# The experts' loops turned round: weight units outside, token pairs inside, both layers by seven products

## The chip, the cores and the metric

The program runs on one core of a Trainium2 chip. The metric is the device time in microseconds (us) of one execution; the time of before is the median of three runs. The trace belongs to one profiled execution. Names: PE in a row is TensorE's matmuls and PEld its weight loads, DVE is VectorE, ACT is ScalarE, POOL is GpSimd, SP is the engine whose queue issues every DMA of this program.

## The reference

Pooled attention over four batches, a dense layer pair with g = h cos h, and a mixture of eight experts whose token weights P come out of eight rounds of row and column normalization:

```python
k_p = k.reshape(B, H, Sp, pool, D).mean(axis=3)      # B, H, S, D = 4, 8, 576, 64; pool = 8
v_p = v.reshape(B, H, Sp, pool, D).mean(axis=3)
attn = softmax(scale * q @ k_p.T); x = (attn @ v_p)  # x: 2304 tokens x 512
h = x @ w_in; x = (h * np.cos(h)) @ w_out            # d_ff = 2048
logits = x @ w_gate; P = np.exp(logits - logits.max())
for _ in range(8):
    P /= P.sum(1, keepdims=True) + 1e-09
    P /= P.sum(0, keepdims=True) + 1e-09
    P *= N / E
for e in range(E):                                   # E = 8, F = 1024
    out += P[:, e:e + 1] * (np.maximum(x @ w1[e], 0.0) @ w2[e])
```

## The kernel before, in words

Every large product is made to fp32 accuracy out of three matmuls in the rounded fp32r type: each operand is cut into a high piece (a rounding copy on ScalarE) and a low piece (source minus high, on VectorE or GpSimd; `halves`), and high x high, high x low and low x high are added in PSUM. Tokens lie in six blocks of 384 (`NB`), and in the experts two blocks make one of three **pairs** (0, 1, 2). The experts' weights lie in 16 **units** (`NU`): half an expert, 512 hidden columns of `w1` and the rows of `w2` that belong to them. One pair through one unit is a **step**; there are 48.

Layer one of a step is a Strassen-Winograd product: seven products P1 to P7 in the order `ORDER`, for two halves h of the unit, each product 6 matmuls of 128x384 (`first_layer`, L1148 before, L1132 after). They need seven combinations of the weights (`w1_pieces`) and seven of the tokens (`x_pieces`), each with a high and a low piece. Layer two goes two ways before: `plain_layer` (L1267) multiplies with the eight plain products, 24 matmuls of 128x256 for each of six token tiles, and `strassen_layer` (L1287) uses seven products, 42 matmuls for each of three tile pairs, but needs seven combinations of the hidden values (`strassen_result`) and of `w2` (`w2_pieces`). VectorE adds the result into `acc` (`accumulate`).

The loops before: pairs outside, units inside. Pair 0 runs through all 16 units with layer two plain; on the way `w1_pieces` and `w2_pieces` make the seven combinations of every unit and store them to DRAM (`w1c`, `w2c`). Pairs 1 and 2 run through all units with layer two by seven products and read 14 + 14 pieces of 256 KB back in each step (`w1_cached`, `w2_cached`). The token pieces of a pair are made once at its start and stay in SBUF.

A planner (`Graph.schedule`) writes the order of each engine's instructions: every node has costs, a due time (`goal`, from which `latest` works back) and buffers from pools of named slots; the order on each engine is fixed once the program is built, and on the chip each engine runs its list in order and waits on semaphores. The string `STRASSEN` says how the 14 products of layer one (`a`) are mixed with those of layer two of the step before it (`0`, `1`, `2`: the three tile pairs).

Ahead of the experts come the attention and the dense layers (`hidden1`, `output1`), in which a weight piece of float64 input is converted by a chain of VectorE instructions, and the pooled keys and values of batches 1 to 3 are made by halving additions on VectorE and GpSimd (`load_k`, `load_v`: `kr`, `ks`, `vr`, `vs`). The gate's logits (`logits`: `pl`, then `pq`) and the normalization (`normalization`: `rw`, `cs`, `pc`, `cr`) are mixed into the end of the dense layers and the start of the experts.

Of the kernel before, what the change touches and what calls it, by code (L numbers as in the profile page):

```python
# [20 lines left out]
POOL = 8  # L21
# [42 lines left out]
class Slot:  # L64

    def __init__(self, tag):
        self.tag, self.free, self.holder, self.kinds = tag, 0.0, None, []


class Group:  # L70

    def __init__(self, graph, name, side, after=()):
        self.graph, self.name, self.side, self.after = graph, name, side, after
        self.kinds, self.pools, self.stack, self.users, self.closed = [], {}, None, 0, False

    def ready(self):
        return self.stack is not None or all(g.users == 0 for g in self.after)
# [14 lines left out]
class Kind:  # L92

    def __init__(self, group, pool, slots, strict=False):
        self.group, self.pool, self.slots, self.strict = group, pool, slots, strict
        self.queue = []
# [18 lines left out]
class Graph:  # L115
# [8 lines left out]
    def group(self, name, side="left", after=()):  # L124
        return Group(self, name, side, after)

    def kind(self, group, pool, names, strict=False):
        group.pools.setdefault(pool, None)
        slots = [self.slots.setdefault((pool, n), Slot(n)) for n in names]
        return Kind(group, pool, slots, strict)  # L130
# [7 lines left out]
    def add(self, engine, us, run, reads=(), writes=(), port=False, table=None, size=0, goal=FAR, name=None):  # L138
# [5 lines left out]
        for items, write in ((reads, False), (writes, True)):  # L144
            for item in items:
# [8 lines left out]
                if buf not in node.bufs:  # L154
                    node.bufs.append(buf)
                    buf.left += 1
                    if buf.kind:
                        buf.kind.group.users += 1
# [15 lines left out]
    def rank(self):  # L174
        self.latest()
        for node in self.nodes:
            if node.engine == ("PE",):
                continue
            for buf in node.bufs:
                store = node.engine == ("SP",)  # L180
                if buf.kind and (store or buf.kind.pool == "ps"):
# [5 lines left out]
        self.latest()  # L187
        for node in self.nodes:
            for buf in node.new:
                buf.first = min(n.late for n, _, _ in buf.acc)  # L190
                buf.kind.queue.append(buf)
                for slot in buf.kind.slots:
                    if buf.kind not in slot.kinds:
                        slot.kinds.append(buf.kind)
        for kind in {id(b.kind): b.kind for n in self.nodes for b in n.new}.values():
            kind.queue.sort(key=lambda b: b.first)

    def place(self, node):

        at, taken = 0.0, []  # L200
        for buf in node.bufs:
# [3 lines left out]
            if not kind.group.ready():  # L205
                return None
# [5 lines left out]
            for slot in kind.slots:  # L212
                if slot.holder is None and slot not in taken and (best is None or slot.free < best.free) and all(
# [9 lines left out]
    def schedule(self, log=None):  # L223
# [25 lines left out]
        while left:  # L249
# [38 lines left out]
            for buf in node.bufs:  # L288
# [3 lines left out]
                kind.group.open()  # L292
                kind.queue.remove(buf)
                slot = slots.pop(0)
                slot.holder, buf.slot = buf, slot
                buf.tile = kind.group.pools[kind.pool].tile(buf.shape, buf.dtype, tag=f"{kind.pool}{slot.tag}", name=buf.name)
# [13 lines left out]
            for buf in node.bufs:  # L310
                buf.left -= 1
                buf.end = max(buf.end, end)
                if buf.kind:
                    buf.kind.group.users -= 1
# [17 lines left out]
    def stuck(self, ready):  # L332
        kinds = {id(b.kind): b.kind for n in self.nodes for b in n.new}
        for k in kinds.values():
            if all(x.holder for x in k.slots):
                print(k.pool, [x.tag for x in k.slots], [(x.holder.name, x.holder.left) for x in k.slots],
# [39 lines left out]
def fused_kernel(ctx: ExitStack, tc: tile.TileContext, qT, kT, vT, v0, wa1, wb1, wa2, wb2, wg, out):  # L376
# [3 lines left out]

    base = g.group("base")
# [4 lines left out]
    late = g.group("late", "right", (second,))  # L386
    plain = g.group("plain", "left", (second,))
    last = g.group("last", "left", (plain, first))
    psum = g.group("psum")

# [6 lines left out]
    xtag = {n: g.kind(base, "xp", [n], True) for n in [f"{p}{j}" for j in range(NBLK) for p in ("xh", "xl")]}  # L397
    k_raw64 = g.kind(base, "xp", ["xh4", "xl4", "xh5", "xl5"], True)
    k_w = many(base, "wp", 19, True)
    k_raw = many(first, "rawp", 3, True)  # L400
    k_gh, k_gl = many(first, "gph", 6), many(first, "gpl", 6)
    k_acc = many(second, "accp", 4)
# [8 lines left out]
    k_gc = {n: g.kind(mid, "gc", [n]) for n in ("ones", "wgr", "wg2", "sel", "lg", "pr")}  # L411
    k_sk = {n: g.kind(mid, "sk", [n]) for n in ("lt", "m1", "m2", "nm", "rw", "cs", "cr")}
    k_tmp = many(mid, "tmp", 4)
    k_s5, k_c22, k_t5 = many(late, "cps", 2), many(late, "cpc", 1), many(late, "cpt", 3)
    k_w2 = many(late, "wp2", 18, True)
    k_gh2, k_gl2 = many(plain, "gph2", 7), many(plain, "gpl2", 7)
    GB = 18
    k_gbh, k_gbl = many(last, "gbh", GB), many(last, "gbl", GB)

# [37 lines left out]
    x1f_tile = dram.tile([NBLK, P, KC, NB], F32, name="x1f")  # L457
    w1c = dram.tile([NU, len(ORDER), P, 2, 2, HD], F32, name="w1c")
    w2c = dram.tile([NU, len(ORDER), 2, P, FU], F32, name="w2c")
    kept_wa = {(u, i, k): g.kept(None) for u in range(U1) for i in range(2 * FC) for k in range(2)}  # L460
    kept_x = {j: g.kept(None) for j in range(NBLK)}
    kept_w1 = {(u, n, k): g.kept(None) for u in range(NU) for n in ORDER for k in range(2)}
    kept_w2 = {(u, n, k): g.kept(None) for u in range(NU) for n in ORDER for k in range(2)}
# [80 lines left out]
    def pool_first_v(tiles):  # L544
# [12 lines left out]
        vpool[0] = vs  # L557

    def load_k(b):
        ks = buf(k_ks, [P, HP, SP], F32, "ks")  # L560
# [4 lines left out]
        kbd = kbds[b % 2]  # L565
        for j in range(2):
            activate(HP * SP, lambda j=j: kbd[j * D:(j + 1) * D, :, j * SP:(j + 1) * SP],
                     lambda j=j: ks[j * D:(j + 1) * D], reads=[ks], writes=[kbd])
        kpool[b] = kbd

    def load_v(b):
        vs = buf(k_vs, [SP, H, D], F32, "vs")
# [45 lines left out]
    x1 = {}  # L618
# [171 lines left out]
    def output1(j, u, c, gs, w, acc, nxt):  # L790
# [17 lines left out]
        if nxt:  # L808
            halves(NB, a, (acc, c), lambda k: nxt[k][:, c, :], [(t, c) for t in nxt])
            if j > 1:  # L810
                load(lambda: x1f_tile[j, :, c], a, P * NB * 4, reads=[(acc, c)], writes=[(kept_x[j], c)])
# [29 lines left out]
    accs, weights, waiting = {}, {}, []  # L841
# [6 lines left out]
    for task, (gi, u, j) in enumerate(tasks):  # L848
# [17 lines left out]
        if u == 0:  # L866
            accs[j] = buf(k_acc, [P, KC, NB], F32, "acc")
# [7 lines left out]
        if u == U1 - 1:  # L875
            x1[j] = x_tiles(j)
        waiting += [lambda c=c, j=j, u=u, gs=gs, w=w, a=accs[j]: output1(
            j, u, c, gs, [w[FC + f] for f in range(FC)], a, x1[j] if u == U1 - 1 else None) for c in range(KC)]
# [4 lines left out]
    gate = {n: buf(k_gc[n], s, d, n) for n, s, d in (  # L883
        ("ones", [P, P], F32), ("wgr", [P, KC, E], F32), ("wg2", [P, KC, P], F32R), ("sel", [G2 + E, E], F32),
        ("lg", [P, NT, E], F32), ("pr", [P, NT, E], F32))}
    ones, wgr, wg2, sel, lg, pr = (gate[n] for n in ("ones", "wgr", "wg2", "sel", "lg", "pr"))
    add("V", 0.17, lambda: nc.vector.memset(ones.tile, 0.0 + 1.0), [], [ones])
    load(lambda: wgr.tile, lambda: wg, P * KC * E * 4, writes=[wgr])
    add("G", 0.6, lambda: nc.gpsimd.memset(wg2.tile.bitcast(F32), 0.0), [], [wg2], port=True)
    activate(KC * E, lambda: wg2[:, :, :E], lambda: wgr.tile, reads=[wgr], writes=[wg2])  # L890
    add("V", 0.2, lambda: nc.vector.tensor_tensor(out=wg2[:, :, G2:G2 + E], in0=wgr.tile, in1=wg2[:, :, :E].bitcast(F32),
                                                  op=ALU.subtract), [wgr], [wg2], port=True)
    add("V", 0.17, lambda: nc.vector.tensor_tensor(out=sel.tile, in0=ident.tile[:G2 + E, :E],
                                                   in1=ident.tile[:G2 + E, G2:G2 + E], op=ALU.add), [], [sel], port=True)
# [4 lines left out]
    def logits(j, goal):  # L899

        pl = buf(b_g, [P, NB], F32, "pl")

        def run():
            for c in range(KC):
                for part in range(2):
                    nc.tensor.matmul(out=pl.tile, lhsT=wg2[:, c, :], rhs=x1[j][part][:, c, :],
                                     start=(c + part == 0), stop=(c == KC - 1 and part == 1))

        lt = sk("lt", [G2 + E, NB])
        pe(mm(2 * KC, NB), run, [wg2, *x1[j]], [pl, (lt, "room")], goal=goal)  # L910
        add("V", two(NB), lambda: nc.vector.tensor_copy(out=lt.tile, in_=pl[:G2 + E, :]), [pl], [lt])
        pq = buf(b_g, [P, TPB, E], F32, "pq")

        def turn():
            for i in range(TPB):
                nc.tensor.matmul(out=pq[:, i, :], lhsT=lt[:, i * P:(i + 1) * P], rhs=sel.tile, start=True, stop=True)

        pe(0.4, turn, [lt, sel], [pq], goal=goal + 3.5)
# [508 lines left out]
```

## Time and profile before

| | |
|---|---|
| time, median of 3 runs | 1992.84 us (1992.48 to 1993.19) |
| the profiled execution, its own time | 1993.46 us, its span 1991.7 us |
| busy in the span | PE 1942.5 us, PEld 1910.8, DVE 1427.6, ACT 961.4, POOL 284.1 |
| start (attention, dense layers) | to about 526 us |
| pair 0, units 0 to 15 | about 526 to 1052 us |
| pairs 1 and 2 | about 1052 to 1992 us |
| HBM read, written | 331.89 MB, 142.08 MB |

A busy PE is not PE at its peak, since matmuls overlap; how fast it goes is read from the distance of their starts. The profiled execution's own time is 1.8 us over its span and 0.6 us over the median.

### The profile page before, as it was taken

Reading aid. Unit: us, or ns where it says so; the run is one execution under the profiler, and the core shown is the slowest. Engines: PE = TensorE matmul, PEld = TensorE weight load, DVE = VectorE, ACT = ScalarE, POOL = GpSimd, SP = SyncE. Lnnn points to the kernel's source line nnn. Section 1 sums busy time; section 2 is a strip of 40 time slices with the busy share of each in tenths; the row PEclk is TensorE's granted clock in tenths of the full one; section 3 lists DMA queues with packets and bytes.
Section 4 is the critical chain, followed back from the end, with each engine's and each line's share of the span. In section 5 each row is a group of like instructions: output and inputs, shape, how many; then the busy total and the mean of one; then the engine's idle time right before and its main releaser. Section 6 shows DMA issues by size and latency. Waiting matters only on the chain.

```text
span 1991.7 us, 35651 instructions
## 1 busy us (share of the span) xinstructions
PE 1942.5 (98%) x13220; PEld 1910.8 (96%) x13220; DVE 1427.6 (72%) x2625; ACT 961.4 (48%) x2026; POOL 284.1 (14%) x249
## 2 busy tenths in 40 slices
PE   6799999999999999999999999999999999999998
PEld 4689999999999999999999999999999999999998
DVE  8898887645688877787776666666667666666666
ACT  6565445643444444444444445445445445444543
POOL 3452232200234232212120000000000000000000
PEclk9799999999999999999999999999999999999999
DMA  7447643334597988989888677678668667767863
GB/s 265 148 154 251 203 149 110 112 118 138 190 316 268 331 296 296 312 295 316 286 314 303 231 260 269 226 251 279 230 240 303 242 234 269 258 230 258 272 223 119
DMA packets 276461, 476.35 MB, mean 239 GB/s; under 512 B 27680, under 2 KB 90912, under 8 KB 276288
## 3 DMA queue, kind: packets, MB, share of 16 engines
q1 hardware_dynamic: 276288, 474.08, 69.5%
q8 instruction: 104, 1.70, 0.4%
q14 instruction: 69, 0.57, 0.1%
HBM read 331.89 MB, written 142.08 MB: 238 GB/s over the span
## 4 chain that ended last, share of the span: by engine, by line
PE 93%; DVE 5%; ACT 1%; DMA 1%; issue 0%; SPq 0%; DVEq 0%; ACTq 0%
PE py L1148 15%; PE pc L1287 13%; PE po L1267 13%; PE qc L1287 10%; PE px L1148 10%; PE pv L1148 10%; PE po L765 3%; PE ph L765 3%; PE po L767 3%; PE ph L766 3%; PE ph L767 3%; PE po L766 3%; PE psc L590 1%; DVE at L449 1%; PE ptr L684 1%; PE px L698 1%
## 5 line engine op out<-in xcount | busy, mean ns | idle before, releaser
L1287 PE MATMUL pc<-wc,gh 128*128 128x256 f32 x1536 | 280.5, 279 | 0.0
L1287 PEld LDWEIGHTS pc<-wc,gh 128*128 128x128 f32 x1536 | 238.2, 188 | 0.0
L1148 PE MATMUL py<-xc,wc 128*128 128x384 f32 x1152 | 232.0, 336 | 0.7 <-ACT py L442 0.7
L1287 PE MATMUL qc<-wc,gh 128*128 128x256 f32 x1152 | 215.6, 280 | 1.1 <-DVE qc L449 1.1
L1287 PE MATMUL pc<-wc,gl 128*128 128x256 f32 x768 | 214.6, 279 | 0.0
L1148 PEld LDWEIGHTS py<-xc,wc 128*128 128x128 f32 x1152 | 197.8, 188 | 1.4 <-ACT py L442 0.9
L1287 PEld LDWEIGHTS qc<-wc,gh 128*128 128x128 f32 x1152 | 186.5, 188 | 2.6 <-DVE qc L449 1.7
L449 DVE TENSOR_TENSOR gl<-sf,gh 128x384 fp32r<-128x384 f32 x256 | 137.6, 551 | 58.3 <-ACT gh L442 55.7
L1287 PE MATMUL qc<-wc,gl 128*128 128x256 f32 x576 | 161.8, 281 | 0.0
L1148 PE MATMUL pv<-xc,wc 128*128 128x384 f32 x768 | 154.6, 336 | 0.0
L1148 PE MATMUL px<-xc,wc 128*128 128x384 f32 x768 | 154.3, 335 | 0.0
L1267 PE MATMUL po<-vhi,gh 128*128 128x256 f32 x768 | 152.0, 279 | 0.7 <-DVE acc L1251 0.7
L1267 PE MATMUL po<-vlo,gh 128*128 128x256 f32 x768 | 152.1, 280 | 0.0
L1267 PE MATMUL po<-vhi,gl 128*128 128x256 f32 x768 | 151.7, 279 | 0.0
L1287 PEld LDWEIGHTS pc<-wc,gl 128*128 128x128 f32 x768 | 144.3, 188 | 0.0
L765 PE MATMUL po<-gh,wc 128*128 128x384 f32 x384 | 132.5, 345 | 7.0 <-ACT wc L442 7.0
L765 PE MATMUL ph<-xh,wc 128*128 128x384 f32 x384 | 133.0, 346 | 3.7 <-DVE r L449 3.7
L767 PE MATMUL ph<-xh,wc 128*128 128x384 f32 x384 | 130.8, 341 | 0.8 <-DVE wc L449 0.8
L766 PE MATMUL ph<-xl,wc 128*128 128x384 f32 x384 | 130.8, 341 | 0.1
L767 PE MATMUL po<-gh,wc 128*128 128x384 f32 x384 | 129.8, 338 | 0.8 <-DVE wc L449 0.8
L1148 PEld LDWEIGHTS pv<-xc,wc 128*128 128x128 f32 x768 | 130.4, 188 | 0.0
L1148 PEld LDWEIGHTS px<-xc,wc 128*128 128x128 f32 x768 | 130.2, 188 | 0.0
(209 smaller groups left out, 4588.9 us busy)
## 6 DMA issues: line engine op xcount, KB each, us to landing
wc<-w1c SPq DMA_DIRECT2D x448, 256.0 KB, 5.2
wc<-w2c SPq DMA_DIRECT2D x448, 256.0 KB, 5.4
wc<-wac SPq DMA_DIRECT2D x112, 256.0 KB, 4.9
w1c<-whi SPq DMA_DIRECT2D x112, 256.0 KB, 4.4
w1c<-wlo SPq DMA_DIRECT2D x112, 256.0 KB, 4.2
w2c<-vhi SPq DMA_DIRECT2D x112, 256.0 KB, 5.0
w2c<-vlo SPq DMA_DIRECT2D x112, 256.0 KB, 4.1
raw<-wa SPq DMA_DIRECT2D x48, 512.0 KB, 5.6
```

What stands on the lines that cost most here:

```text
L449: (nc.gpsimd if e == "G" else nc.vector).tensor_tensor(out=out(), in0=in0(), in1=in1(), op=op)
L590: nc.tensor.matmul(out=ps[off:off + n, 2 * hh:2 * hh + 2, :].rearrange("p h s -> p (h s)"), lhsT=qc()[:, hh, off:off + n], rhs=kpool_at[b] ...
L684: nc.tensor.transpose(ps[:, h, :], at[:, i, h, :], ident.tile)
L698: nc.tensor.matmul(out=px[e * D:(e + 1) * D, off:off + n], lhsT=vs[b][:, 2 * hp + e, :], rhs=pt[:, 2 * hh + e, off:off + n], start=True, s ...
L765: nc.tensor.matmul(out=ps, lhsT=lh, rhs=rh, start=(i == 0), stop=False)
L766: nc.tensor.matmul(out=ps, lhsT=lh, rhs=rl, start=False, stop=False)
L767: nc.tensor.matmul(out=ps, lhsT=ll, rhs=rh, start=False, stop=(i == total - 1))
L1148: nc.tensor.matmul(out=ps(), lhsT=l[:, k], rhs=r[:, c, :], start=(start and c + n == 0), stop=(c + n == 3), skip_group_check=True)
L1267: nc.tensor.matmul(out=po[:, d * HD:(d + 1) * HD], lhsT=l[:, r], rhs=w[f % 2, d][k][:, (f // 2) * HD:(f // 2 + 1) * HD], start=(f + n + d ...
L1287: nc.tensor.matmul(out=ps, lhsT=l[:, r], rhs=m[:, k], start=(start and h + n == 0), stop=(h + n == 3), skip_group_check=True)
```

## The change

1. The loops are turned round: units outside, pairs (1, 0, 2) inside. `w1_pieces` and `w2_pieces` run once for a unit and their 14 + 14 pieces stay in SBUF for three steps, in exactly 14 + 14 slots (`W1`, `W2`), so the next unit's pieces take the slots one by one as the last step lets go of them. Nothing of the weights is stored or reloaded.
2. All 48 steps use `strassen_layer`; `plain_layer` is gone. The output sums of all three pairs stay in SBUF (`k_acc2`).
3. The seven token pieces of each pair are stored to DRAM (`xc`, 768 KB each) and read again in every step but the first, into 7 slots (`x_loaded`).
4. The logits are fp32 matmuls of 8 columns straight out of `acc`, 12 for each block, in place of 8 fp32r matmuls of 384 columns, a copy and 3 small matmuls.
5. Keys and values of batch 1 are pooled on TensorE (`ON_PE`: `pk`, `pv`).
6. The planner works its due times out four times over, counting when a slot's next holder comes; slots of several pools can be joined; the dense layers' weights get 21 slots for 19.

```diff
+    W1, W2, GB, XR, T5 = 14, 14, 12, 7, 2
+    k_x = g.kind(base, "xp", xnames[:XR], True)
+    k_w1 = many(base, "wp", W1, True)
+    k_w = g.join(k_w1, many(second, "wq", 7), strict=True)
+    k_w2 = many(ahead, "wp2", W2, True)
...
+        if b in ON_PE:
+            tiles = load_rows(k1[ON_PE.index(b)])
+            pk = buf(b_a, [P, HP, SP], F32, "pk")
...
+                        nc.tensor.matmul(out=pk[:, hp, :], lhsT=t[:rows, i, hp * P:(hp + 1) * P], rhs=band[:rows, o:o + SP],
+                                         start=(c == 0), stop=(c == len(tiles) - 1))
...
-            for c in range(KC):
-                for part in range(2):
-                    nc.tensor.matmul(out=pl.tile, lhsT=wg2[:, c, :], rhs=x1[j][part][:, c, :],
...
+            for i in range(TPB):
+                for c in range(KC):
+                    nc.tensor.matmul(out=pl[:, i, :], lhsT=accs[j][:, c, i * P:(i + 1) * P], rhs=wgr[:, c, :],
...
         cut("P1", a11)
+        cut("P4", a22)
+        combine(a22, a21, a22, ALU.add)
+        cut("P5", a22)
+        combine(a21, a11, a21, ALU.subtract)
+        combine(a22, a22, a11, ALU.subtract)
+        cut("P6", a22)
         cut("P2", a12)
         cut("P7", a21)
+        combine(a12, a12, a22, ALU.subtract)
         cut("P3", a12)
-    def w1_cached(u):
...
+    def x_loaded(pair):
+        x = {}
+        for name in ORDER:
+            t = buf(k_x, [P, 2, 2, NB], F32R, "xc")
+            load(lambda t=t: t.tile.bitcast(F32), lambda name=name: xc[pair, ORDER.index(name)], P * 4 * NB * 4,
+                 reads=[kept_x[pair, name]], writes=[t])
...
-    def plain_layer(pair, u, gs, w, acc2, goals):
...
-    steps = [(pair, u) for pair in range(NTP) for u in range(NU)]
+    steps = [(u, pair) for u in range(NU) for pair in (1, 0, 2)]
...
+    for n, (u, pair) in enumerate(steps):
+        if pair == steps[0][1]:
+            w1, w2 = w1_pieces(u), w2_pieces(u)
+        pieces = {}
+        first_layer(w1, ready if n == 0 else x_loaded(pair), strassen_result(pieces), goals1[n])
+        own = {2: (b_x, b_y)} if n == len(steps) - 1 else None
+        strassen_layer(pair, u, pieces, w2, boxes[pair], goals2[n], own)
```

Over the whole program the built lists differ by this: matmuls 13,044 before and 12,787 after; layer two 6,336 matmuls of 128x256 before and 6,048 after; layer one 4,032 of 128x384 in both. DMAs 1,725 before and 709 after.

Three places in the lists. **TensorE, a step of pair 0 before**: a product of layer one (`py`), then the start of a plain group, whose three rows stand four times in all (24 matmuls):

```order
L1148 MATMUL py<-xc,whi 128x384 x2
L1148 MATMUL py<-xc,wlo 128x384
L1148 MATMUL py<-xc,whi 128x384 x2
L1148 MATMUL py<-xc,wlo 128x384
L1267 MATMUL po<-vhi,gh 128x256 x2
L1267 MATMUL po<-vlo,gh 128x256 x2
L1267 MATMUL po<-vhi,gl 128x256 x2
```

After, a step of pair 0 on the same engine: the product of layer one is the same, and what follows is one product of layer two by seven (6 matmuls).

```order
L1132 MATMUL py<-xc,whi 128x384 x2
L1132 MATMUL py<-xc,wlo 128x384
L1132 MATMUL py<-xc,whi 128x384 x2
L1132 MATMUL py<-xc,wlo 128x384
L1228 MATMUL pc<-vhi,gh 128x256
L1228 MATMUL pc<-vlo,gh 128x256
L1228 MATMUL pc<-vhi,gl 128x256
L1228 MATMUL pc<-vhi,gh 128x256
L1228 MATMUL pc<-vlo,gh 128x256
L1228 MATMUL pc<-vhi,gl 128x256
```

The weights are read as the same kind of pieces in both; 24 matmuls for a tile have become 42 for two.

**VectorE, a step of pair 1 before**, where no weights are made (`pv`, `c`: sums of layer one; `gl`: low pieces of hidden values; `pc`, `qc`: sums of layer two):

```order
L449 TENSOR_TENSOR pv_17904<-py,s_17929 128x384
L449 TENSOR_TENSOR gl<-sf,gh 128x384 x2
L1125 SCALAR_TENSOR_TENSOR gl<-px_17875,gh 128x384
L449 TENSOR_TENSOR c_17994<-py,s_17929 128x384
L449 TENSOR_TENSOR pc<-qc,t_17965 128x256
L449 TENSOR_TENSOR gl<-c_17994,gh 128x384
L1209 SCALAR_TENSOR_TENSOR spare<-pv_17904,c_17994 128x384
```

After, in the last step of a unit, the same sums with the next unit's weight pieces (`raw`: combinations in place; `wlo`: low pieces) among them:

```order
L469 TENSOR_TENSOR pv_12124<-py,s_12146 128x384
L469 TENSOR_TENSOR raw<-raw 128x512
L469 TENSOR_TENSOR wlo<-raw,whi 128x512
L469 TENSOR_TENSOR raw<-raw 128x512
L469 TENSOR_TENSOR wlo<-raw,whi 128x512
L1109 SCALAR_TENSOR_TENSOR gl<-px_12115,gh 128x384
L469 TENSOR_TENSOR c_12223<-py,s_12146 128x384
L469 TENSOR_TENSOR wlo<-raw,whi 128x512
L469 TENSOR_TENSOR pc<-qc,t_12190 128x256
L469 TENSOR_TENSOR wlo<-raw,whi 128x512
L1177 SCALAR_TENSOR_TENSOR spare<-pv_12124,c_12223 128x384
```

From this `pv` to the unit's eighth weight row VectorE has 24 rows: 12 of 128x384, 8 of the weights (128x512), 2 of `acc` (128x512) and 2 of 128x256. Over a unit it has 17 weight rows and GpSimd 5, where before they stood in pair 0's steps alone.

**SP's queue, pair 1 before**, each piece 256 KB:

```order
L454 DMA wc1_13114<-w1c_124 128x512 [waits DMAHW6_49,PE_49]
L454 DMA wc1_13121<-w1c_124 128x512 [waits DMAHW7_49,PE_49]
L454 DMA wc2_13134<-w2c_125 128x512 [waits DMAHW0_49,PE_49]
L454 DMA wc2_13140<-w2c_125 128x512 [waits DMAHW1_49]
L454 DMA wc2_13155<-w2c_125 128x512 [waits DMAHW2_49,PE_49]
```

After, the last two token pieces of a step, the next unit's sources, and the first of the next step:

```order
L474 DMA xc_12253<-xc_144 128x1536 [waits DMAHW1_49,PE_49]
L474 DMA xc_12287<-xc_144 128x1536 [waits DMAHW2_49,PE_49]
L474 DMA raw2_12327<-wb2 128x1024 [waits DVE_49]
L474 DMA raw2_12328<-wb2 128x1024 [waits DMAHW3_49,DVE_49,Pool_49]
L474 DMA raw_12374<-wa2 128x1024 [waits DMAHW4_49,DVE_49]
L474 DMA xc_12516<-xc_144 128x1536 [waits DMAHW5_49,PE_49]
```

Twenty-eight reloads of a step have become seven larger ones, and sources that wait for VectorE and GpSimd stand ahead of the next step's token pieces in the one queue.

## Rows read from the trace of the kernel before

**Rows 1.** The page: busy time, share of the span and instructions of each engine.

```profile
PE 1942.5 (98%) x13220; PEld 1910.8 (96%) x13220; DVE 1427.6 (72%) x2625; ACT 961.4 (48%) x2026; POOL 284.1 (14%) x249
```

**Rows 2.** Windows: stretch; busy (instructions) of PE, PEld, DVE, ACT, POOL; clock, DMA share, GB/s.

```profile
25.00:150.00 125.00, 101.43 (x572) 87.67 (x573) 112.84 (x204) 77.63 (x131) 61.94 (x69) 0.89 0.54 167
640.00:1054.00 414.00, 413.59 (x3021) 413.26 (x3020) 312.17 (x473) 179.06 (x347) 95.51 (x65) 1.00 0.89 307
1523.00:1970.00 447.00, 447.00 (x3198) 446.52 (x3197) 295.19 (x579) 217.50 (x491) 0.00 (x0) 1.00 0.71 245
```

**Rows 3.** Waits of TensorE from 560 to 1960 us, the longest (total, times, longest).

```profile
PE py L1148 <- ACT py L442: 0.7, 1, 0.7
```

**Rows 4.** Timeline of TensorE in pair 1: start, length, what, count.

```profile
1102.26 1.20 PE L1148 MATMUL px<-xc,wc 128*128 128x384 f32 x6
1103.30 0.40 PE L1287 MATMUL qc<-wc,gh 128*128 128x256 f32 x2
...
1104.00 0.39 PE L1287 MATMUL pc<-wc,gh 128*128 128x256 f32 x2
```

**Rows 5.** The chain that ended last: a plain group of pair 0 (start, length).

```profile
667.18 2.80 PE po L1267 x24
```

**Rows 6.** Timeline of VectorE in pair 2, GpSimd idle.

```profile
1823.02 0.55 DVE L449 TENSOR_TENSOR sf<-spare 128x384 f32<-128x384 f32 x1
1823.49 0.74 DVE L1251 SCALAR_TENSOR_TENSOR acc<-pc,pr,acc 128x512 f32<-128x512 f32 x1
1824.15 0.42 DVE L449 TENSOR_TENSOR qc<-qc,t 128x256 f32<-128x256 f32 x1
```

**Rows 7.** Groups of VectorE and GpSimd, 610 to 1000 us (busy, mean ns, idle before).

```profile
L449 DVE TENSOR_TENSOR vlo<-raw,vhi 128x512 fp32r<-128x512 f32 x33 | 23.6, 734 | 0.0
L449 DVE TENSOR_TENSOR s<-raw 128x512 f32<-128x512 f32 x4 | 2.7, 684 | 0.0
L449 POOL TENSOR_TENSOR wlo<-raw,whi 128x512 fp32r<-128x512 f32 x20 | 26.6, 1332 | 49.8 <-ACT whi L442 34.1 <-PE pv L1148 14.4 <-DMA w1c<-whi 1.1
```

**Rows 8.** Timeline of VectorE at the start of pair 0, GpSimd busy.

```profile
565.42 1.78 DVE L449 TENSOR_TENSOR s<-raw 128x512 f32<-128x512 f32 x1
```

**Rows 9.** Timeline of TensorE: the gate's small fp32 matmuls, and what follows.

```profile
515.64 0.83 PE L916 MATMUL pq<-sel,lt 40*128 40x8 f32 x6
516.41 0.44 PE L765 MATMUL po<-gh,wc 128*128 128x384 f32 x1
```

**Rows 10.** Timeline of TensorE: the first step of pair 0.

```profile
541.99 0.62 PE L1148 MATMUL py<-xc,whi 128*128 128x384 f32 x2 [1.35 <-DVE pv L449]
...
549.42 0.62 PE L1148 MATMUL py<-xc,whi 128*128 128x384 f32 x2 [2.47 <-DVE c L449]
...
554.51 0.52 PE L1148 MATMUL px<-xh,whi 128*128 128x384 f32 x1
554.83 0.52 PE L1148 MATMUL px<-xl,whi 128*128 128x384 f32 x1
```

**Rows 11.** Windows: TensorE's clock after those waits.

```profile
552.00:558.00 6.00, 5.58 (x18) 5.58 (x19) 4.16 (x12) 2.43 (x5) 0.25 (x1) 0.51 0.67 248
```

**Rows 12.** Timeline of TensorE at the start: pooled values of batch 0, and what follows.

```profile
12.78 4.71 PE L552 MATMUL pv<-v,band 128*72 128x512 f32 x10
17.43 0.63 PE L684 MATMUL ptr<-ident,at 128*72 128x128 f32 x4
```

**Rows 13.** Groups of VectorE to 150 us: a halving addition of the pooling.

```profile
L449 DVE TENSOR_TENSOR vs<-vr 72x128 f32<-72x128 f32 x5 | 2.8, 597 | 0.0
```

**Rows 14.** Timeline of VectorE: one round of the normalization, from `cr` to `cr`.

```profile
613.89 0.16 DVE L949 TENSOR_SCALAR cr<-pc 128x8 f32<-128x8 f32 x1
...
616.89 0.17 DVE L949 TENSOR_SCALAR cr<-pc 128x8 f32<-128x8 f32 x1
```

**Rows 15.** DMA from 1100 to 1500 us, and a reload of 256 KB (us to landing).

```profile
DMA packets 54201, 99.11 MB, mean 248 GB/s; under 512 B 6014, under 2 KB 6014, under 8 KB 54166
...
wc<-w2c SPq DMA_DIRECT2D x192, 256.0 KB, 5.4
```

More of the change, by code (lines that the diff above doesn't have):

```diff
@@ L92, with __init__ @@
 class Kind:
-    def __init__(self, group, pool, slots, strict=False):
-        self.group, self.pool, self.slots, self.strict = group, pool, slots, strict
-        self.queue = []
+    def __init__(self, slots, strict=False):
+        self.slots, self.strict, self.queue = slots, strict, []
+        self.groups = list({id(s.group): s.group for s in slots}.values())
+        self.psum = slots[0].pool == "ps"
 class Buf:
@@ L157, in add @@
                     if buf.kind:
-                        buf.kind.group.users += 1
+                        for group in buf.kind.groups:
+                            group.users += 1
         node.wait = len(deps)
@@ L186, in rank @@
                             node.goal = min(node.goal, other.late + max(other.us) + (6.0 if store else 2.0))
[L187 to L196, printed above, removed]
+        for n in range(4):
+            self.latest()
+            kinds = {}
+            for node in self.nodes:
+                for buf in node.new:
+                    buf.first = min(x.late for x, _, _ in buf.acc)
+                    kinds.setdefault(buf.kind, []).append(buf)
+            for kind, queue in kinds.items():
+                queue.sort(key=lambda b: b.first)
+                kind.queue = queue
+                for slot in kind.slots:
+                    if kind not in slot.kinds:
+                        slot.kinds.append(kind)
+            for kind, queue in kinds.items():
+                if n < 3 and all(slot.kinds == [kind] for slot in kind.slots):
+                    for buf, heir in zip(queue, queue[len(kind.slots):]):
+                        for node, _, _ in buf.acc:
+                            if node.engine != ("PE",):
+                                node.goal = min(node.goal, heir.first - max(node.us))
     def place(self, node):
@@ L212, in place @@
             for slot in kind.slots:
-                if slot.holder is None and slot not in taken and (best is None or slot.free < best.free) and all(
+                if slot.holder is None and slot not in taken and slot.group.ready() and (best is None or slot.free < best.free) and all(
                         k is kind or not k.queue or k.queue[0].first >= buf.first for k in slot.kinds):
@@ L385, in fused_kernel @@
     mid = g.group("mid", "right", (early,))
-    late = g.group("late", "right", (second,))
-    plain = g.group("plain", "left", (second,))
-    last = g.group("last", "left", (plain, first))
+    late = g.group("late", "right", (early,), mid)
+    ahead = g.group("ahead", "right", (early,), late)
+    more = g.group("more", "left", (second,))
     psum = g.group("psum")
+    ON_PE = (1,)
     const = ctx.enter_context(tc.tile_pool(name="const", bufs=1))
```

384 lines of the change are left out of this document (144 added, 240 removed).

## The prediction

> **What bounds the kernel now.** I read the page first: TensorE is busy for 98% of the span [rows 1]. A busy TensorE need not be at its peak, so the windows come next. From 640 to 1054 us and from 1523 to 1970 us it is busy for 413.59 of 414 and 447.00 of 447 us at granted clock 1.00, VectorE for 75% and 66% [rows 2]. Then the list of its waits: from 560 to 1960 us the longest is 0.7 us [rows 3]. So over 70% of the run goes at the pace at which matmuls follow each other, and only the number of columns counts there. That pace is read from starts in the timeline: six matmuls of 384 columns take 1102.26 to 1103.30, 0.1737 us each, and six of 256 columns 1103.30 to 1104.00, 0.1167 us each [rows 4]; a plain group of 24 takes 2.80 us, the same 0.1167 [rows 5]. A step of pair 0 is therefore 84 x 0.1737 + 144 x 0.1167 = 31.4 us, and one of pairs 1 and 2 84 x 0.1737 + 126 x 0.1167 = 29.3 us. The first 150 us are another matter: TensorE idles there for 23.6 of 125 us at clock 0.89, and VectorE is busy for 112.84, 90% [rows 2]: it sets the pace. And the first step of pair 0 loses time in waits and at a low clock [rows 10, 11].
>
> **The change part by part.** The sum is made against the profiled execution's 1993.46 us, 0.6 us over the median.
>
> *Layer two of pair 0 by seven products.* 16 steps lose 18 matmuls each, 288 in all: 288 x 0.1167 = **-33.6 us**. TensorE waits for nothing there [rows 2, 3], so the matmuls are on the path themselves. The other matmuls of the experts are the same in number and form.
>
> *Logits.* Out go 48 matmuls of 384 columns (8.3 us) and 18 small fp32 matmuls. In the trace three such are six passes, and the next matmul starts 0.77 us after the first of them [rows 9]: 0.128 us a pass, 36 passes 4.6 us. In come 72 fp32 matmuls of 8 columns, 144 passes, 18.5 us at that price. Together **+5.5 us**. The row has 40 rows of weights and the new ones 128, so the price is a neighbour's. Below, a pass at half that price would make it -3.7; above, four passes of 128 columns last 0.63 us [rows 12], 0.157 each, and make it +9.7.
>
> *Pooling of batch 1 on TensorE.* Ten passes of 512 columns take 12.78 to 17.43, 4.7 us [rows 12]; the 20 new ones of the keys are 40 passes, 5.1 us at 0.128. TensorE gains 9.8 us of work in a stretch with 23.6 us of idle time. VectorE's list loses some 10 halving additions of at most 0.6 us [rows 13], 6 us, and GpSimd's 13, which also lets go of VectorE (the last part says how). VectorE is the pace there, so I take **-4 us**; -14 if TensorE's idle time shrinks by as much again, +9.8 if nothing that waits for VectorE comes earlier and the new matmuls stand on the path.
>
> *The change of stages at 540 to 558 us.* Waits of 1.35 and 2.47 us for VectorE's `pv` and `c` [rows 10], then 18 matmuls at 0.32 us instead of 0.174 (2.6 us) at clock 0.51, the lower level of 1.2 GHz [rows 10, 11]: 6.4 us lost. The order is planned anew, pieces of weights are made once rather than with a store beside them, and the first pair's combinations come in another order. I take half of it back, **-3 us** (0 to -6.4).
>
> *Normalization.* Its eight rounds run beside the first steps. A round is 3.0 us from `cr` to `cr` [rows 14], a chain on VectorE with one small matmul in it. After, the sums of successive rounds stand only 18 to 26 layer-one matmuls apart on TensorE's list, 3.1 to 4.5 us, so VectorE has 0.1 to 1.5 us to spare for anything else in a round. **+1.5 us** (0 to +5).
>
> *Token pieces streamed.* Seven of 786 KB in 29.3 us are 188 GB/s, and the weights' sources 2.1 MB in three steps, 24: 212 GB/s where 248 went without a wait [rows 15, 3]. In before's pair 1 a reload of 256 KB lands in 5.4 us with 28 of them a step [rows 15]; a piece after is let go of some 11 us before its next holder is due, so the cover is 11 us, and it is gone only if sources stand in the queue waiting for VectorE for that long. SP's queue takes things in turn, and token pieces are queued behind those sources. In the first unit stores go beside the loads. **+1 us** (0 to +5).
>
> *Weights remade at the change of units.* Before, pair 0 made them and stored them, with slots to spare. Now the next unit's 28 pieces take their slots while the last step of the old unit runs, and TensorE waits for `wlo` directly. VectorE's stretch from the `pv` of that step to the eighth weight row is 24 instructions: 12 x 0.47 (distance of starts of 384-column additions), 8 x 0.73 [rows 7], 2 x 0.66 for `acc` and 2 x 0.42 [rows 6], 13.6 us. TensorE has 56 matmuls of 384 and 66 of 256 columns beside it, 9.73 + 7.70 = 17.4 us. So VectorE is 78% full with 3.8 us to spare, and the pieces come in time, if nothing disturbs it. What can is GpSimd: beside it one VectorE addition took 1.78 us [rows 8] where the group's mean is 0.684 [rows 7], 1.1 us more. Five GpSimd rows a unit give up to 5.5 us, more than the spare. But most meet no such VectorE row at the moment it matters: in 640 to 1054 us GpSimd was busy for 95.51 us and TensorE waited for 0.4 [rows 2]. I take 0.2 us at each of 15 changes, **+3 us** (0 to +24, 1.6 each with half of the blocking in excess of the spare).
>
> The Trainium skill, "SBUF — State Buffer", section "Who interferes with whom", has a rule against this part: VectorE and GpSimd share a pair of SBUF ports under an exclusive lock. The 1.78 us beside 0.684 agrees. By that rule taken in full each of the five GpSimd rows would delay VectorE, 5.5 us a unit; the sum above goes by the rows.
>
> Sum: -33.6 + 5.5 - 4 - 3 + 1.5 + 1 + 3 = -29.6; 1993.46 - 29.6 = 1963.9, less the 0.6 between the profiled execution and the median: **1963 us**.
>
> **Rivals.**
> 1. *The gain is given back at the changes of units (slower than before).* VectorE comes late by one wait such as the 2.47 us in the first step, and the clock falls as it did there, so that 18 matmuls cost 2.6 us more [rows 10, 11]: 5.1 us each time, 81 us over 16 units, 1963 - 3 + 81 = 2041. It decides from about 2 us a unit (30/16). For it: VectorE 78% full, single slots. Against: 3.8 us spare, and one such fall in all of the run of before. Chance 0.07. The Trainium skill, "TensorE: Matmul & The Clock Gate", section "HAM oscillation — how this bites in real kernels", describes loops in which every turn waits once and pays for the clock again; the row shows the fall once.
> 2. *The same late VectorE by GpSimd's blocking, without the clock*: 0.8 to 1.6 us a change, 13 to 26 us in place of my 3: 1973 to 1986. For it: [rows 7, 8]; against: the idle cover above. Chance 0.13.
> 3. *The start gives more.* If VectorE's relief reaches TensorE in full, -14 for -4, and the change of stages gives back all 6.4 us, with logits at half price: 1963 - 10 - 3.4 - 9.2 = 1940 at best, 1954 for half of it. Chance 0.19.
> 4. *Nothing comes of it*: the matmuls taken out of pair 0 were cover for something else, so that the time stays within 4 us of before. That would need VectorE or DMA to be the bound in pair 0; at 75% and with 0.4 us of idle TensorE [rows 2] neither is. Chance 0.03.
>
> **How the numbers follow.** The forecast (1954 to 1972) has chance 0.58; rivals 1 to 4 have 0.07, 0.13, 0.19 and 0.03. Rival 2 lies from 1973 to 1986, rival 3 from 1940 to 1954. A range from 1946 to 1981 leaves out rival 1, rival 4, the lower half of rival 3 at most and the last third of rival 2: 0.07 + 0.03 + 0.06 + 0.04 = 0.2. 0.2% is 4 us, about what a measurement of this kernel can tell from no change. Forecast and rivals 2 and 3 are all faster by more than that: 0.90; rival 4 the same: 0.03; rival 1 slower: 0.07.
>
> **What would show it.** Each step: 126 matmuls of layer two in every one, 29.3 us from one step to the next in all three pairs, TensorE busy all through, at clock 1.00. Logits: groups of `pl` with 0.128 us from pass to pass. Start: VectorE still near 90% but the stretch shorter, and `pv`, `pk` rows of TensorE where it idled. Change of units: VectorE 80 to 90% busy in the last step of a unit, waits of TensorE for `wlo` or `gl` of a few tenths; waits over 1 us there, and a clock under 1.00 after them, would say rival 1 or 2. DMA: about 212 GB/s in the steady state, no wait for `xc`. The prediction is wrong if steps after come out longer than 29.3 us without a wait (the pace itself would have changed), or if waits for `xc` show that the queue's order costs what its bandwidth does not.

## The result and the profile after

| | before | after |
|---|---|---|
| time, median (lowest to highest) | 1993.01 us (1992.48 to 1993.96, 4 runs) | 1963.45 us (1959.33 to 1967.99, 4 runs) |
| ratio, 95% interval | | 0.9852 (0.9822 to 0.9882) |
| profiled execution, its span | 1993.46 us, 1991.7 us | 1967.44 us, 1965.4 us |

Faster by 29.6 us; 1963 was forecast. The profiled execution is one of the two longer of its four, and the scatter is itself a finding: 1959.3 and 1959.5 at mean clock 0.991, 1967.4 and 1968.0 at 0.986 and 0.987.

The windows after, with the columns of [rows 2] (the kernel's last matmul ends at 1961.5 us):

```profile
25.00:150.00 125.00, 117.73 (x663) 97.09 (x662) 105.69 (x199) 78.52 (x141) 56.39 (x65) 0.92 0.59 188
640.00:1054.00 414.00, 414.00 (x2960) 413.96 (x2959) 327.98 (x634) 229.93 (x514) 31.18 (x23) 1.00 0.56 207
```

TensorE has filled up the start (117.73 of 125 us for 101.43) and VectorE has come down to 105.69. In this stretch of the experts TensorE is busy all through at clock 1.00, VectorE for 79%. The same matmul of a step stands 29.42 us after that of the step before in the timeline:

```profile
885.95 0.51 PE L1132 MATMUL pv<-xc,whi 128*128 128x384 f32 x2
...
915.37 0.51 PE L1132 MATMUL pv<-xc,whi 128*128 128x384 f32 x2
```

Waits of TensorE from 560 to 1960 us, columns as in [rows 3]: all of them lie before 621 us or behind 1940 us, and no `xc`, `wlo` or `vlo` is among them.

```profile
PE pc L975 <- DVE cs L972: 1.7, 2, 1.1
PE qc L1228 <- DVE qc L469: 1.6, 2, 0.9
PE px L1132 <- ACT py L462: 0.6, 1, 0.6
```

What was not foreseen stands in the dense layers. A group of logits in TensorE's timeline, and windows of it (317.20) and of what follows (319.80), then of the next group (336.10) and what follows:

```profile
317.21 2.74 PE L943 MATMUL pl<-wgr,acc 128*128 128x8 f32 x24
319.81 0.42 PE L814 MATMUL ph<-xh,wc 128*128 128x384 f32 x1
```

```profile
317.20:319.80 2.60, 2.60 (x26) 2.60 (x25) 0.55 (x1) 1.01 (x2) 0.00 (x0) 1.00 0.00 0
319.80:323.20 3.40, 3.40 (x15) 3.40 (x15) 1.21 (x3) 0.52 (x1) 0.00 (x0) 0.62 0.00 0
336.10:338.70 2.60, 2.60 (x26) 2.60 (x24) 2.04 (x3) 1.48 (x3) 0.00 (x0) 1.00 0.09 38
338.80:342.20 3.40, 3.40 (x21) 3.40 (x22) 2.02 (x4) 1.03 (x2) 0.00 (x0) 1.00 0.53 205
...
361.40:368.20 6.80, 6.80 (x32) 5.51 (x32) 2.23 (x5) 1.39 (x3) 1.00 (x1) 0.51 0.01 2
```

The 24 passes take 2.60 us, 0.108 each, and TensorE waits for nothing in the group or just before it; yet behind the group the clock is at its lower level (1.2 of 2.4 GHz) for about 3.4 us, behind the second group it is not, behind the third for 6.8 us. In this profile four of six groups are followed by such a stretch, 17.1 us in all, half of it lost: 8.5 us. Only ahead of the fourth group does TensorE wait, for 1.2 us in all. The kernel before, whose logits are matmuls of 384 columns, keeps the upper level from 310 to 530 us, over a wait of 0.7 us in the attention too:

```profile
310.00:530.00 220.00, 219.28 (x1305) 213.23 (x1304) 134.27 (x255) 106.83 (x206) 27.52 (x26) 1.00 0.36 115
```

The other place is the end of the first unit, where rounds of the normalization and remade weight pieces meet. VectorE there, with an addition of 1.65 us (from start to start 0.47 is usual, [rows 6]); GpSimd, which is busy beside it; and TensorE's waits and clock:

```profile
612.73 1.65 DVE L469 TENSOR_TENSOR sf<-spare,sf 128x384 f32<-128x384 f32 x1
614.30 0.68 DVE L1208 COPY acc<-pc 128x512 f32<-128x512 f32 x1
614.90 0.42 DVE L469 TENSOR_TENSOR qc<-qc,t 128x256 f32<-128x256 f32 x1
```

```profile
612.48 1.49 POOL L469 TENSOR_TENSOR wlo<-raw,whi 128x512 fp32r<-128x512 f32 x1 [0.88 <-ACT whi L462]
```

```profile
615.38 0.39 PE L1228 MATMUL qc<-vhi,gh 128*128 128x256 f32 x1 [0.94 <-DVE qc L469]
...
617.02 0.39 PE L975 MATMUL pc<-cs,ones 128*128 128x8 f32 x2 [0.67 <-DVE cs L972]
```

```profile
604.00:610.00 6.00, 4.94 (x34) 4.74 (x34) 5.58 (x16) 2.76 (x7) 0.00 (x0) 1.00 0.85 323
610.00:618.00 8.00, 6.38 (x41) 5.79 (x41) 7.49 (x18) 5.84 (x13) 2.78 (x2) 0.97 0.96 378
618.00:624.00 6.00, 5.43 (x17) 4.93 (x17) 4.46 (x12) 1.87 (x4) 0.37 (x1) 0.50 0.11 44
```

### The profile page after: what moved, and what is told of

Same layout as the page of the kernel before. It is cut to its first block, busy times and chain, and to the rows that moved or that the text cites. A ratio compares the mean times of both kernels' runs of the same rounds, so it can differ in the third digit from the quotient of the medians.

```text
span 1965.4 us, 34055 instructions
## 1 busy us (share of the span) xinstructions
PE 1934.5 (98%) x13042; PEld 1900.3 (97%) x13042; DVE 1509.9 (77%) x2911; ACT 1064.0 (54%) x2310; POOL 247.5 (13%) x222
## 4 chain that ended last, share of the span: by engine, by line
PE 95%; DVE 3%; DMA 1%; ACT 1%; issue 0%; SPq 0%; POOL 0%; ACTq 0%
PE pc L1228 20%; PE qc L1228 15%; PE py L1132 15%; PE px L1132 10%; PE pv L1132 10%; PE po L814 3%; PE po L815 3%; PE po L816 3%; PE ph L814 3%; PE ph L815 3%; PE ph L816 3%; PE px L747 1%; PE pl L943 1%; PE psc L640 1%; PE ptr L733 1%; DVE at L469 1%
## 5 line engine op out<-in xcount | busy, mean ns | idle before, releaser
L1228 PE MATMUL pc<-vhi,gl 128*128 128x256 f32 x1152 | 321.9, 279 | 0.1
L1228 PE MATMUL pc<-vhi,gh 128*128 128x256 f32 x1152 | 321.6, 279 | 0.0
L1228 PE MATMUL pc<-vlo,gh 128*128 128x256 f32 x1152 | 321.6, 279 | 0.0
L1132 PE MATMUL py<-xc,whi 128*128 128x384 f32 x1152 | 294.1, 336 | 0.0
L1228 PE MATMUL qc<-vhi,gh 128*128 128x256 f32 x864 | 242.8, 281 | 3.0 <-DVE qc L469 2.8
L1228 PE MATMUL qc<-vhi,gl 128*128 128x256 f32 x864 | 241.6, 280 | 0.5 <-DVE gl L469 0.5
L1228 PE MATMUL qc<-vlo,gh 128*128 128x256 f32 x864 | 241.0, 279 | 0.0
L1228 PEld LDWEIGHTS pc<-vhi,gl 128*128 128x128 f32 x1152 | 216.4, 188 | 0.5 <-DVE gl L469 0.5
L1228 PEld LDWEIGHTS pc<-vlo,gh 128*128 128x128 f32 x1152 | 216.7, 188 | 0.0
L1228 PEld LDWEIGHTS pc<-vhi,gh 128*128 128x128 f32 x1152 | 215.7, 187 | 0.0
L1132 PE MATMUL py<-xc,wlo 128*128 128x384 f32 x576 | 193.3, 336 | 0.0
```

The source lines that it names most:

```text
L1132: nc.tensor.matmul(out=ps(), lhsT=l[:, k], rhs=r[:, c, :], start=(start and c + n == 0), stop=(c + n == 3), skip_group_check=True)
L1228: nc.tensor.matmul(out=ps, lhsT=l[:, r], rhs=m[:, k], start=(start and h + n == 0), stop=(h + n == 3), skip_group_check=True)
```

## The experiments

**The changed kernel again.** 

> The changed kernel once more, unaltered. Its four executions lay at 1959.3, 1959.5, 1967.4 and 1968.0 us with mean granted clocks of 0.991, 0.991, 0.986 and 0.987, and the profiled one (1967.4) shows TensorE's clock at 0.50 for 2 to 7 us behind four of the six groups of gate logits, with no wait of TensorE there. Theory A (the falls behind the logits decide which of the two times an execution gets): again two clusters 8 us apart, and if the profile falls on a short execution, fewer low stretches behind the groups of logits and nothing else different. Rival B (the 8 us come from the start or from the first steps of the experts): the profile of a short execution has the low stretches behind the logits and differs elsewhere.

 Measured: 1958.3, 1959.5, 1964.2, 1964.6, 1970.9 us at mean clocks 0.992, 0.991, 0.988, 0.988, 0.985: not two clusters but a spread that goes with the clock. Its profile (1964.6) has a low stretch behind five of the six groups of logits, 20.5 us, and none at 618 us, though TensorE's waits there are the same. So the two clusters of A did not come, and between the two profiles the falls behind the logits do not decide: the shorter execution has more of them, and gains by a low stretch at the start that is 3.4 us shorter and by the clock at 618 us. That there are falls behind the logits is confirmed; the scatter has several places.

**Logits in pieces of two.**

```diff
-        pe(TPB * KC * 0.115, run, [wgr, accs[j]], [pl], goal=goal)
...
+        for n in range(0, TPB * KC, 2):
+            add("PE", 2 * 0.22, lambda n=n: run(n // KC, range(n % KC, n % KC + 2)), [wgr, accs[j]], [pl],
+                goal=goal, name="pl")
...
-                s.est = max(s.est, end + (0.0 if same else self.SIGNAL[e]))
+                s.est = max(s.est, end + (2.0 if node.name == s.name == "pl" else 0.0 if same else self.SIGNAL[e]))
```

> Only the order on TensorE is altered: the 12 matmuls of 8 columns of each block are emitted two at a time, some 2 us of dense-layer matmuls apart, instead of 12 in a row. Work is the same, every matmul is still there. Theory A: no low stretch between 310 and 530 us, all executions in one cluster near the lower one of the changed kernel, about 1958 to 1960 us, so 4 us below its median of 1963.5. Rival B: the clock is not set by the run of short passes; the time stays at 1959 to 1968 with both clusters. Rival C: each switch to an 8-column matmul and back costs more than in a row (36 switches at 0.1 to 0.2 us for 6): 3 to 6 us are given back and the time does not fall.

 Measured: median 1957.9 us (1955.8 to 1969.7). In its profile (1965.6) the falls behind the logits are gone but for one at 364 to 374 us, in a row of short matmuls of the attention with a wait of 1.3 us. But the order behind it was laid anew as well: at the rounds TensorE now waits 2.0 us at worst, and the clock falls there. Each switch back to 384 columns costs 0.09 us (0.26 from start to start where 0.174 is usual), 2.7 us for 30 more. Its median is 6.3 us below that of the run before it (1964.2, the changed kernel on the same chip, called the control from here on), but the times overlap and the one cluster of theory A did not come: mixed as a verdict.

**Rounds later.** `goal=clock["t"] + 40.0 + 11.0 * n` for `5.0 * n`. 

> The eight rounds of the normalization are due 11 us apart instead of 5, so that they no longer meet the first unit change; work is the same. In the changed kernel TensorE waits there four times between 604 and 621 us (1.06, 0.94, 0.67, 0.56 us) and its clock is 0.50 from 618 to 624 us: together about 6 us. Theory A (VectorE is full there because rounds and remade weight pieces coincide): these waits and the low clock go, the time falls by 4 to 6 us against the changed kernel in either cluster. Rival B (the remake of weight pieces alone makes VectorE late at the first unit change): the waits stay at the unit change, less than 2 us gained.

 Measured: median 1953.6 us (1952.7 to 1960.6). From the first priming matmul (`pset`, which marks the start of the experts) to the end of the span it is 1426.4 us, where the two profiles of the changed kernel have 1431.7 and 1428.8: 2.4 us of waits, and 2.9 more where the clock fell too. A holds for the four waits; a wait of 1.7 us at 608 us, for `gl`, is left. The rest of the gain was luck at the start: TensorE's list is the same up to `pset`, but the pooled keys ran at the other clock. The windows over these passes in the profile with later rounds and (second fence) in the changed kernel's profile:

```profile
28.30:34.00 5.70, 5.70 (x42) 5.11 (x44) 5.00 (x9) 1.58 (x4) 2.03 (x2) 1.00 0.79 266
```

```profile
28.70:37.40 8.70, 8.70 (x42) 7.77 (x42) 5.04 (x9) 1.60 (x3) 2.73 (x2) 0.60 0.66 229
```

The first dense matmul comes at 38.2 us there and at 44.4 here.

**Pair 0 at 144 matmuls again.** `mms(q0(), "P4", i)` twice when `pair == 0`. 

> In the 16 steps of pair 0 the last product of layer two is multiplied twice, which brings its count from 126 back to the 144 matmuls of the plain form; it changes the result (that product is added twice). Theory A (these matmuls are on the path, 0.1167 us each): 288 x 0.1167 = 33.6 us more than the changed kernel, 31 to 36 with its scatter. Rival B (VectorE or the streamed token pieces already set part of the pace of a step): the added matmuls hide behind that, less than 25 us more.

 Measured: median 1995.7 us (1988.4 to 2003.4, 10 runs), 31.5 us over the control on the same chip; from `pset` to the end 1461.2 us, 32.4 over the control's 1428.8, 0.113 a matmul. Theory A: what was taken out of pair 0 was on the path. Neither this profile nor the control's has a fall at 618 us.

**Both edits of the order.** 

> Both edits of the order together: logits two matmuls at a time and rounds due 11 us apart; the work is that of the changed kernel. The kernel with later rounds alone gave 1952.7 to 1960.6 us (median 1953.6), and its profile still has the low clock behind three of six groups of logits, 13.7 us at 0.50, which is 6.8 us lost. Theory A: these go, so 1946 to 1950 us where the clock at the start is as in that profile, up to 6 us more where the 40 passes of pooled keys run at 0.50. Rival: 36 switches to 8-column matmuls cost 0.1 to 0.2 us each and take back 4 to 7 us: 1952 to 1956 us.

 Measured: median 1958.6 us (1949.2 to 1964.0). The profiled one (1958.6) has the slow start; up to `pset` it gains only 2.0 us on the changed kernel's profile: one fall is left at 366 to 373 us, and waits for reloaded dense weights (1.1 and 0.2 us) and of 1.3 us have come in. From the 1248th matmul of the dense layers to `pset` it takes 225.7 us, where the profile with later rounds alone has 225.6: what the clock gave back, the switches and the new waits took. So the rival holds in this profile, though the median lies above the times that either expected.

**No pooling on TensorE.** `ON_PE = ()`. 

> Keys and values of batch 1 are pooled by halving additions on GpSimd and VectorE as in the kernel before; the rest is the changed kernel. The 576th dense matmul starts 6.6 us earlier in the changed kernel than in the one before. Theory A (the pooling on TensorE bought that): the start is as late as before, so the time is 3 to 7 us above the changed kernel's 1958 to 1971. Rival B (the gain comes from the other alterations of the start, 21 weight slots and the newly ranked order, and the 60 passes on TensorE are themselves a loss): the same time or up to 5 us less, and the scatter is smaller, because the 40 short passes of the keys, which ran at 0.53 in one profile and at 1.00 in another, are gone.

 Measured: median 1966.3 us (1965.3 to 1970.0), 2.1 us over the control, which ran on another chip. In its profile the 576th matmul of the dense layers starts at 193.3 us, in the changed kernel's two at 188.8 and 187.2, before at 195.4. So pooling on TensorE is worth 4.5 to 6.0 us where the pooled keys run largely at the low clock, as in both profiles of the changed kernel, and the other edits of the start 2.2. Theory A by the trace; the medians show 2.1 of the 3 to 7 us expected. The smaller scatter that the rival expected came too: 4.7 us for the control's 12.6.

**No remake of the weight pieces.** `if n == 0:` ahead of `w1, w2 = w1_pieces(u), w2_pieces(u)`, with later rounds. 

> With the rounds later as above, and the weight pieces of unit 0 used for all 16 units: units 1 to 15 are neither loaded nor cut, which leaves out their weights (the result is that of a mixture with one repeated unit). Theory A (the remake hides wholly in VectorE's spare time once the rounds are out of its way): within 2 us of the kernel with later rounds at an equal mean clock. Rival B (each change of units costs a few tenths, as the 3 us of the prediction had it): 3 us or more faster at an equal clock. Rival C (the blocking by GpSimd costs 0.8 us or more at each change): 12 us or more faster.

 Measured: median 1956.8 us (1949.0 to 1959.5). From `pset` to the end 1423.1 us against 1426.4 with the remake: 3.2 us. Of these 2.4 lie in the first two units, 1.7 of them in the one wait at 608 us (first change of units), which is gone; the steady units take 88.20 us for some 88.26, under 0.1 us a change. The sum is B's, but not its few tenths at each change; C is out.

**A quarter of the logits.** `for c in range(1)`, with later rounds. 

> With the rounds later, and the gate's logits taken from the first 128 of 512 columns only: 3 matmuls (6 passes) for each block in place of 12 (24 passes), in the same places of the same order; the result is that of another gate. The 108 passes left out take 0.108 us each at full clock, 11.7 us. Theory A (a row of 24 short passes lets the clock fall): the low stretches behind the groups go as well, so 11.7 + 3 to 9 us, 15 to 21 us less than the kernel with later rounds. Rival B (the low stretches have another cause that comes at the same places): 10 to 13 us less, and the low stretches stay.

 Measured: 1942.5, 1943.8, 1944.3 and 1950.2 us. Its profile (1943.8) has the slow start too, the first dense matmul at 44.1 us. Behind the first and the fifth of its groups, where the changed kernel's profile falls to the lower level:

```profile
317.10:323.90 6.80, 6.80 (x40) 6.80 (x40) 4.13 (x9) 2.62 (x6) 0.00 (x0) 1.00 0.00 0
...
506.40:513.20 6.80, 6.80 (x41) 6.80 (x41) 4.31 (x8) 2.41 (x5) 0.00 (x0) 1.00 0.00 0
```

The other four are at 1.00 as well. Its base, the kernel with later rounds, has low stretches behind three groups in one profile and two in the other, 13.7 us in both, so 6.8 lost. From the 1248th matmul of the dense layers to `pset` those two take 225.6 us each, this one 211.2: 14.4 less. Five groups of 18 passes fewer at 0.108 us are 9.7. So 4.7 us more than the passes came back, beside 1.2 us of a new wait: theory A in this profile. It is one profile; the execution of 1950.2 us, at mean clock 0.990 where the others have 0.993 and 0.994, lost more to the clock somewhere.

**Rounds later, again.** 

> The kernel with rounds due 11 us apart once more, unaltered, as the base for the next two on the same chip; so far 1952.7, 1953.0, 1954.2 and 1960.6 us, the profiled one with the 40 passes of pooled keys at clock 1.00 (first dense matmul at 38.2 us, 44.1 to 44.7 us in five other profiles of the same order). Expected 1952 to 1961 us; a profile with the first dense matmul near 44 us should stand some 6 us higher than one near 38 us at equal falls behind the logits.

 Measured: 1955.3, 1960.5, 1961.5, 1968.2 us, mean clocks 0.993 to 0.986; the profile is the 1955.3, first dense matmul at 39.2 us. The upper end lies above what was expected; the median, 1961.0, is near the changed kernel's. Over both runs the eight executions with later rounds have a median of 1957.9 us, the nine of the changed kernel 1964.2, and the two spreads overlap. One edit of the order of this size is therefore read from its stretch of the trace, not from four executions.

**Keys pooled as the values are.**

```diff
+            pe(4.7, run, [band] + [(t, i) for t, i, _ in tiles], [pw], goal=FAR)
+            activate(DM, lambda: kw.tile, lambda: pw.tile, reads=[pw], writes=[kw], from_psum=True)
+            pe(0.6, turn, [ident, kw], [pk], goal=FAR)
```

> On top of the later rounds, the keys of batch 1 are pooled as the values are: 5 matmuls of 512 columns, one copy on ScalarE, and 4 transposes of 72x128, in place of 20 matmuls of 72 columns; the same result. Ten passes of 512 columns took 4.6 us, four short matmuls some 0.6 us, against 5.6 us of the 40 passes at clock 1.00 and 8.8 us at 0.53. Theory A (the 40 short passes draw the clock down, by chance of when they fall): first dense matmul near 38 us in the profile, and no execution above 1957 us but for the falls behind the logits; median 1950 to 1954. Rival B (the clock at 30 to 50 us is low because of TensorE's waits before, at 10 to 20 us): the low stretch stays, the time is that of the kernel with later rounds, within 2 us.

 Measured: 1958.1 to 1961.1 us, median 1958.3. The scatter is down from 13 to 3 us, but the first dense matmul is at 40.9 us, and the clock is low before and behind the new wide matmuls, not in them (windows before, over and behind them):

```profile
20.00:28.00 8.00, 7.86 (x14) 2.93 (x14) 7.04 (x16) 3.04 (x6) 0.73 (x2) 0.63 0.67 224
28.00:32.70 4.70, 4.70 (x12) 1.31 (x12) 4.63 (x10) 1.79 (x3) 0.00 (x0) 1.00 0.80 239
32.70:41.00 8.30, 6.02 (x30) 3.34 (x29) 7.00 (x14) 4.56 (x9) 1.27 (x1) 0.70 1.02 373
```

A's first dense matmul near 38 us and its median did not come, and a low stretch stays, as B had it, with a median 2.7 us under that of its base. That the 40 short passes made the scatter fits these five times; that the waits of the start make the low clock is not shown.

**The same, logits in pieces of four.** 

> The same, and the logits emitted four matmuls (8 passes) at a time some 2 us apart, 18 pieces instead of 36 of two or 6 of twelve. Theory A: most of the low stretches behind the logits go (5 to 9 us back) for 12 more switches at about 0.09 us (1 us): 1944 to 1950 us. Rival: as with pieces of two, other things move in the newly laid order (waits for converted weights and for the attention at 360 to 370 us), and the median is not below that of the kernel with wide keys alone.

 Measured: 1950.9, 1950.9, 1954.4 and 1958.3 us, median 1952.65; ratio to the kernel before 0.981 (0.9794 to 0.9827), below the control's 0.9858 (0.9836 to 0.9879). From 150 to 540 us its clock is 1.00, the changed kernel's 0.98:

```profile
150.00:540.00 390.00, 388.26 (x2314) 382.30 (x2313) 271.28 (x496) 191.82 (x362) 73.36 (x63) 1.00 0.48 161
```

Its profile has no low stretch from 103 us to the end of the experts. This version does the whole of the work and beats both kernels, and wide keys alone by 5.6 us on the same chip, so the rival is out; it falls short of the 1944 to 1950 us expected, by about what one new wait takes:

```profile
552.07 0.61 PE L1140 MATMUL px<-xc,whi 128*128 128x384 f32 x2 [2.43 <-DVE gl L1117]
```

The clock did not fall behind this wait.

## Why the prediction was right, term by term

The mechanism was right: the matmuls taken out of pair 0 were on the path, and the changes of units did not give the gain back. That the sum came out to 0.5 us is luck: the terms missed on both sides, and the changed kernel's own executions lie up to 12.6 us apart. Against the changed kernel's profile (span shorter by 26.3 us):

- *Layer two of pair 0*, -33.6: right. Put back, it costs 31.5 to 32.4 us. A step is 29.42 us where 29.3 was worked out, and pairs 1 and 2 of before were at 29.37 (from the same matmul of one step to the next), so most of the 0.1 us was there before.
- *Logits*, +5.5: the step that failed. The pass was priced too high (0.108 us for 0.128: 15.6 - 12.9 = +2.7), and what a row of short passes does to the matmuls behind it was not priced at all: 8.5 us in this profile. Together +11.2, above the upper bound of 9.7. With three quarters of the passes out, the low stretches were gone as well in the one profile taken.
- *Pooling on TensorE* and the start, -4: measured -6.4 at the 1248th dense matmul (312.9 to 306.5 us), and -14.0 in the profile whose keys ran at full clock, the lower bound that was given. The price of 0.128 us for a pass of the keys is 0.141 at full clock and 0.217 in the changed kernel's profile.
- *Change of stages*, -3: the waits of 1.35 and 2.47 us and the low clock [rows 10, 11] are gone; two waits of 0.17 and 0.48 us stand in their place, so about -5.8.
- *Normalization*, +1.5: 3.2 us of waits (1.06, 0.94, 0.67, 0.56) and 6 us at 0.50, about +6, beyond the +5 given. Rounds alone were priced. The remade pieces of the first change of units stand in the same stretch, and VectorE was full there (7.49 of 8 us); spacing the rounds took 2.4 to 5.3 us back, and the wait that was left went with the remake. How much of it GpSimd caused is not shown beyond the one row of 1.65 us.
- *Token pieces*, +1: no wait for `xc`, 0. The DMA moved 211 GB/s from 578 to 1900 us; 212 was worked out.
- *Remade weights*, +3: 3.2 us with the rounds out of the way, but over half of it at the first change; the other 14 cost under 0.1 us each. In the changed kernel's profile the first change stands in the line above, so about +1.0 here.

-32.4 + 11.2 - 6.4 - 5.8 + 6 + 0 + 1.0 = -26.4. This is an account, not a proof of each size: two more waits of before (0.49 and 0.60 us at 551 to 553 us), which are gone, are not in it. Rival 1, the clock falling at a change of units, is there once, at 618 us, and in one of two profiles. Its condition, a late VectorE that takes the clock with it, is not a rule here: single waits of 1.70 and 2.43 us in the later versions were not followed by a fall. Rival 2 did not come, though GpSimd did hold VectorE up at later changes as well: an addition of a usual 0.55 us takes 0.94 to 1.00 beside it at each of the 14, and TensorE waits for nothing there, so the spare covered it.

```profile
825.70 0.95 DVE L469 TENSOR_TENSOR gl<-sf,gh 128x384 fp32r<-128x384 f32 x1
```

```profile
824.93 1.30 POOL L469 TENSOR_TENSOR raw<-raw,raw 128x512 f32<-128x512 f32 x1 [1.65 <-DVE vlo L469]
```

The Trainium skill's rule ("SBUF — State Buffer", "Who interferes with whom") agrees with these rows and with that of 1.65 us. Rival 3's start came in the two profiles of the kernel with later rounds alone, not in those of the changed kernel.

## What to carry to other kernels

When a wide matmul is replaced by many narrow ones, price the stretch behind them as well: look at the granted clock there even where TensorE never waits, and mix the narrow ones into wide work, a few at a time. Two chains that each fit in VectorE's spare time do not fit if they are due in the same stretch: add up what stands there, not each by itself. And where executions of one kernel differ with the mean clock, judge an edit of the order from its own stretch of the trace, since a handful of times can show the start's luck.

## What the runs showed of the hardware that was not expected

A row of 24 fp32 passes of 8 columns, 2.6 us with TensorE busy all the time, was followed by 3.4 to 10.2 us at the lower clock in two to five of six places, not always the same ones in two executions of one program: 28 of 48 places over the eight profiles that have such rows, and never behind the sixth. Six passes in the same places were not followed by one in the one profile taken, nor were pieces of eight, once two in a row, in the one profile that has them. Forty passes of 72 columns ran at 1.00 in the two profiles of the kernel with later rounds alone (5.6 us) and at 0.60 on the mean in the changed kernel's (8.7 us); in seven of the nine profiles with the same list on TensorE up to there the mean is 0.57 to 0.71. The Trainium skill, "TensorE: Matmul & The Clock Gate", "HAM oscillation — how this bites in real kernels", tells of falls behind gaps in which TensorE waits; at the first group shown here there was no such gap. What decides in which execution a place falls is left open.
